# Delta-rule attention followed by a SiLU feed-forward: the output projection by seven products of blocks in place of eight, and what is moved for it

## The chip, the cores and the metric

The kernel runs on one core of a Trainium2 chip. The metric is the device time of one execution in microseconds; lower is better. Before the change it is 801.19 us, the median of three runs (799.85 to 801.63). The engines are called PE (TensorE), DVE (VectorE), ACT (ScalarE), POOL (GpSimd) and SP (the engine whose queue issues all DMAs here).

## The reference

There are 4 sequences (B), 8 heads (H), 768 tokens (S) and heads of 48 (D). For every sequence and head a 48x48 state is carried through the tokens:

```
k_n = k / (norm(k) + 1e-6);  state = 0
for t in range(S):
    y[t]  = q[t] @ state
    v_old = k_n[t] @ state
    state = state + beta[t] * outer(k_n[t], v[t] - v_old)
```

The outputs of the 8 heads of a token stand side by side (8 x 48 = 384) and go through a feed-forward, with w_in of 384x2048 and w_out of 2048x384:

```
h = x @ w_in
g = h * sigmoid(h)
out = g @ w_out            # 3072 x 384
```

Inputs and output are float32, but w_in and w_out reach the kernel as float64.

## The kernel before

**Tiling.** The 768 tokens are cut into 6 chunks of 128, and a chunk of one sequence is a unit; the 24 units are counted chunk by chunk. A chunk goes through four stages:

- *Preparation* (`prepare`), sequence by sequence: k and q are transposed on PE (`turn`, L369), scores are made from them (`score`, L392), scaled and masked on ACT and DVE into the tile `ap` (L402, L408), and the diagonal 32x32 blocks go out to DRAM and come back in another layout (`g`, L436 and L444). Then k is scaled into `bkb` and v in place, both on POOL.
- *Inversion* (`invert`): the 32x32 triangular blocks of all heads are inverted together on DVE, 30 steps of two instructions (L470, L474), each needing the one before. The result goes out (`up`, `low`, L485) and comes back into `xe` and `xi` (L488).
- *Solve* (`solve`): small products on PE merge the blocks and solve for Z (`zbufs`), update the state (`pu`) and give the outputs (`pyc`), in ten steps over the four sequences that overlap each other. DVE adds into `vf` (L558), updates the state (L616) and ACT and DVE copy `xT`, the transposed input of the feed-forward; its last rows come by six small DMAs a sequence (L653).
- *Feed-forward* (`feed_forward`), for each half of the chunk (two sequences): `hidden` makes 8 times two blocks of 128 hidden features for 256 tokens (L702), with SiLU on ACT into `gT` (L712); `project` then makes the output of each sequence from 16 blocks (L722), which ACT scales by 0.5 (L728) and SP stores (L730). The products of both use a pool of two PSUM banks (`psM`).

**Order.** The order of each engine's instructions is written out by hand: `pin` orders each compute instruction behind the one before it on its engine, and `in_line` does so for all DMAs, which share one queue of SP. So an instruction that waits holds up everything emitted after it on its engine. The feed-forward of chunk c is a generator, `pieces`; each step of it is a piece (three blocks of L702 or two of L722). The main loop runs preparation, inversion and solve of chunk c + 1 and takes pieces of chunk c in between, so that PE has work while the other engines make the next chunk. The last chunk's feed-forward stands alone at the end. Squares and norms of the k of chunk c + 2 (`squares`, `norms`, on ACT and DVE) are emitted behind solve of chunk c + 1.

**Weights.** A weight comes in as raw float64 and is narrowed to float32 in three steps on ACT, DVE and POOL (`narrow`, L164 to L180). There are eight pieces of w_in and eight of w_out. A raw piece needs a place of 6 KB a partition: the halves of `w_outs` not yet written, buffers of `gT`, a tile `spare`, and for pieces 2, 3, 6 and 7 of w_out two of the four buffers of `ap`. `fill`, `until` and `more` deal out the steps while chunk 0 is solved and chunk 1 prepared. `busy` (L274) puts idle products on PE in these stages.

**Buffers.** k has 5 buffers and q 4; q of the next chunk is loaded in preparation (`load_q`, L127), right after the block stores of its sequence. Z has four tiles of its own.

Of the kernel before, what the change touches and what calls it, by code (L numbers as in the profile page):

```python
# [21 lines left out]
def kernel(  # L22
# [85 lines left out]
    NQ, NK, NBK = 4, 5, 5  # L108
    qbufs = [const.tile([P, NP, 2, W], FP32, name=f"qb{i}") for i in range(NQ)]
    kbufs = [const.tile([P, NP, 2, W], FP32, name=f"kb{i}") for i in range(NK)]  # L110
    bkbufs = [const.tile([P, NP, 2, W], FP32, name=f"bkb{i}") for i in range(NBK)]
    vfs = {}
# [12 lines left out]
    def load_q(i):  # L125
        if i < N:
            in_line(nc.sync.dma_start(out=packed(qbufs[i % NQ]), in_=chunk_of(q, i)))  # L127
# [8 lines left out]
    for t in kbufs[:B] + qbufs:  # L136
        pin(nc.vector.memset(t[:, :, :, D:W], 0.0))
# [60 lines left out]
    def fetch_w_in(i):  # L198
        if i < 4:
            raw = room(1 - i // 2, i % 2)  # L200
        elif i < NWI - 1:
            raw = mlp.tile([P, SIZE], U32, name="raw", tag="gT", bufs=3)[:]
        else:
            raw = spare[:]
        raw = raw.rearrange("p (a f) -> p a f", a=NKT)
        for at, row, rows in ROWS:
            step = row(1) - row(0)
            src = moe_w_in[row(0) : row(0) + rows, i * WF : (i + 1) * WF].bitcast(U32)
            pitch = src.ap[0][0]
            src = bass.AP(  # L210
                tensor=src.tensor, offset=src.offset,
                ap=[[pitch, rows], [pitch * step, NKT], [1, 2 * WF]],
            )
            in_line(nc.sync.dma_start(out=raw[at : at + rows], in_=src))
        raws[i] = raw.rearrange("p a (f j) -> p a f j", j=2)

    raws = {}
    spare = const.tile([P, SIZE], U32, name="spare")
# [6 lines left out]
    def fetch_w_out(i):  # L225
        if i in (0, 1, 4):
            raw = room(1, min(i, 1))
        elif i == 5:
            raw = spare[:]
        else:  # L230
            k = i % 2
            if k not in places:
                places[k] = work.tile([P, SIZE], U32, name="raw_out", tag="ap", bufs=4)
            raw = places[k][:]
# [14 lines left out]
    for t in kbufs[B:] + bkbufs:  # L249
        nc.gpsimd.memset(t[:, :, :, D:W], 0.0)  # L250
# [9 lines left out]

    HH = HB * H
    xis = [const.tile([P, HH, W], FP32, name=f"xi{i}") for i in range(2)]
    xe = const.tile([W + T, BH, T], FP32, name="xe")

    zbufs = [const.tile([P, NP, 2, W], FP32, name=f"z{i}") for i in range(B)]
    for t in zbufs:
        nc.gpsimd.memset(t[:, :, :, D:W], 0.0)
# [26 lines left out]
    def squares(c):  # L294

        sums[c] = small.tile([P, BH], FP32, name="ss", bufs=1)[:]
        for b in range(B):
            sq = packed(zbufs[b])
# [59 lines left out]
    def turn(i, *rooms):  # L358

        b, c = units[i]  # L360
        kb, qb = kbufs[i % NK], qbufs[i % NQ]
# [84 lines left out]
    def invert(c):  # L446
# [39 lines left out]

        def move(to, src, j, mine):
            in_line(nc.sync.dma_start(out=to, in_=src[mine, j].rearrange("n s t -> s n t")))  # L488

        for hf in range(2):  # L490
            mine = slice(hf * HH, (hf + 1) * HH)
            for j in range(0, NB, 2):
                move(xe[T * j : T * (j + 1), mine, :], low, j, mine)
# [5 lines left out]
    xTs = {}  # L499

    def solve(c, us):
# [6 lines left out]
        ys, pzs, pys, third = {}, {}, {}, {}  # L508
# [5 lines left out]
        for g in range(2 if c == 0 else 0):  # L514
            thirds = work.tile([P, HB, NKT, 2, W], FP32, name="thirds", tag="gx"[g], bufs=1)
            pin(nc.gpsimd.memset(thirds[:], 0.0))
            for n in range(HB):
                third[g * HB + n] = thirds[:, n]

        def merge(g, second):  # L520
# [3 lines left out]
            for n in range(HB):  # L524
                x = g * HB + n
                for h in range(H):
                    for k in range(2):
                        even, odd = slice(W * k, W * k + T), slice(W * k + T, W * (k + 1))
                        if second:
                            to, left, right = even, ys[g][odd, n * H + h, :], xis[g][odd, n * H + h, T:W]  # L530
# [10 lines left out]
            else:  # L541
                ys[g] = work.tile([P, HH, T], FP32, name="y")
                pin(nc.scalar.copy(ys[g][T:W], pm[T:W]))
                pin(nc.vector.tensor_copy(out=ys[g][W + T : P], in_=pm[W + T : P]))
# [76 lines left out]
        def new(x):  # L621
# [29 lines left out]
            for e in range(2):  # L651
                for a in range(NKT):
# [3 lines left out]
                    ))  # L656

# [38 lines left out]
    def hidden(c, hf):  # L696

        for f in range(NFF // 2):
# [15 lines left out]
            ))  # L714
            yield

    def project(c, b, room=(psM, "m")):

        po = bank(*room, "po")
        for f in range(NFF):  # L720
# [5 lines left out]
            if f == NFF - 1:  # L726
                o = mlp.tile([P, DM], FP32, name="o")
                pin(nc.scalar.mul(o[:], po[:, 0:DM], 0.5))  # L728
                row = b * S + c * C
                in_line(nc.sync.dma_start(out=out[row : row + C, :], in_=o[:]))  # L730
            if f % 2 == 1:
                yield

    def feed_forward(c):
        for hf in range(2):
            yield from hidden(c, hf)
            for b in range(hf * HB, (hf + 1) * HB):
                yield from project(c, b)
# [8 lines left out]
    def prepare(c, us):  # L747

        for b in range(B):
# [7 lines left out]
            load_q(i + NQ)  # L757
            block_in(i)
            load_k(i + B)
            scale(i)  # L760
# [41 lines left out]
    def fill(n):  # L802

        ops = []
        while len(ops) < n and queue:
            piece = queue[0]
            piece.begin()
            if len(queue) > 1 and piece.done >= 2:
# [49 lines left out]
    for n, _ in enumerate(solve(0, us)):  # L858
        fill(2)
        if n == 3:  # L860
            more(2)
            more(3)
        if n == 8:
            more(4, ("out", 1))
# [4 lines left out]
    until(("in", 7))  # L869
    fetch_w_out(5)  # L870
    queue.append(Piece(("out", 5), narrow_w_out(5)))
# [3 lines left out]
    more(6, ("out", 2))  # L875
    more(7, ("out", 3))
    for n in range(2):
        go(prep)
        go(pieces, 3)
        fill(6)  # L880
    for n in range(2):
        until(("out", 6 + n))
        go(prep)
        go(pieces, 2)
    inv = invert(1)
    go(pieces, 6)
    for _ in range(20):
# [4 lines left out]
    go(pieces, 8)  # L892
    for n, _ in enumerate(solve(1, us)):
        go(pieces, 2 if n in (1, 2) else 1)
    squares(2)
    norms(2)
# [5 lines left out]
    for c in range(1, NCH):  # L902
        if c + 1 < NCH:
            us = []
            for n, _ in enumerate(prepare(c + 1, us)):
                go(pieces)
            go(pieces, 4)
            inv = invert(c + 1)
            n = 0
            for _ in inv:  # L910
                n += 1
                if n % 5 in (1, 3, 4):
                    go(pieces)
            go(pieces, 8)
            for n, _ in enumerate(solve(c + 1, us)):
                go(pieces, 2 if n in (1, 2) else 1)
            if c + 2 < NCH:
                squares(c + 2)
                norms(c + 2)
# [35 lines left out]
```

## Time and profile before

| | |
|---|---|
| median of 3 runs | 801.19 us |
| the profiled execution, its own time | 800.27 us |
| its span, from the first to the last instruction | 798.6 us |
| mean granted clock of TensorE | 0.974 |
| busy: PE, weight loads (PEld) | 760.3, 572.2 us |
| busy: DVE, ACT, POOL | 339.4, 231.1, 82.3 us |
| L702 (hidden) | 1152 instructions |
| L722 (output projection) | 768 instructions, for 384 products of 128x128 by 128x384: each product of float32 is two instructions |

The page gives busy times by engine, 40 slices of the span in tenths, and the chain of work that ended last, followed back from the end. A line of a group gives source line, engine, operation, output and inputs with their shapes, the number of instructions, busy time and the mean duration of one, and then the engine's idle time just before such instructions, with what ended it. In the chain in order of time each line has a start, a length and the work; a timeline is the same for one engine, with waits in brackets.

### The profile page before, as it was taken

Reading aid. Unit: us, or ns where it says so; the run is one execution under the profiler, and the core shown is the slowest. Engines: PE = TensorE matmul, PEld = TensorE weight load, DVE = VectorE, ACT = ScalarE, POOL = GpSimd, SP = SyncE. Lnnn points to the kernel's source line nnn. Section 1 sums busy time; section 2 is a strip of 40 time slices with the busy share of each in tenths; the row PEclk is TensorE's granted clock in tenths of the full one; section 3 lists DMA queues with packets and bytes.
Section 4 is the critical chain, followed back from the end, with each engine's and each line's share of the span. In section 5 each row is a group of like instructions: output and inputs, shape, how many; then the busy total and the mean of one; then the engine's idle time right before and its main releaser. Section 6 shows DMA issues by size and latency. Waiting matters only on the chain.

```text
span 798.6 us, 15397 instructions
## 1 busy us (share of the span) xinstructions
PE 760.3 (95%) x6326; PEld 572.2 (72%) x6326; DVE 339.4 (42%) x892; ACT 231.1 (29%) x502; POOL 82.3 (10%) x102
## 2 busy tenths in 40 slices
PE   7449798999999999999999999999999999999998
PEld 5336576678778688768678868678868778767684
DVE  5886779561254732424732424642425732100000
ACT  5533566121234113314113314113314113211020
POOL 5005246100020000030000030000030000000000
PEclk8769998999999999999999999999999999999999
DMA  9798747321025140025140025140022040000000
GB/s 157 119 183 150 178 131 172 77 73 32 15 58 106 36 103 2 12 60 106 37 103 2 10 61 103 40 100 6 10 61 44 16 107 2 11 22 0 21 1 20
DMA packets 155062, 50.85 MB, mean 64 GB/s; under 512 B 142544, under 2 KB 147536, under 8 KB 154992
## 3 DMA queue, kind: packets, MB, share of 16 engines
q1 hardware_dynamic: 154992, 49.87, 30.2%
q8 instruction: 50, 0.82, 0.4%
q14 instruction: 20, 0.16, 0.1%
HBM read 34.70 MB, written 14.16 MB: 61 GB/s over the span
## 4 chain that ended last, share of the span: by engine, by line
PE 83%; DVE 6%; DMA 5%; ACT 2%; SPq 2%; issue 1%; POOL 0%; ACTq 0%; DVEq 0%
PE phid L702 28%; PE po L722 28%; PE pa L392 5%; PE pz L567 4%; PE pw L274 3%; PE pt L369 3%; PE pyc L626 2%; PE ph L551 2%; PE pyc L598 2%; DMA qb<-in_q_dram 2%; PE px L534 2%; PE py L534 2%; PE pu L609 1%; DVE x L474 1%; DVE rank L470 1%
## 5 line engine op out<-in xcount | busy, mean ns | idle before, releaser
L702 PE MATMUL phid<-xT,w_in 128*128 128x256 f32 x1152 | 268.6, 386 | 1.3 <-ACT gT L712 0.8
L722 PE MATMUL po<-w_out,gT 128*128 128x384 f32 x768 | 254.8, 489 | 0.0
L702 PEld LDWEIGHTS phid<-xT,w_in 128*128 128x128 f32 x1152 | 215.0, 191 | 39.3 <-issue 7.0
L722 PEld LDWEIGHTS po<-w_out,gT 128*128 128x128 f32 x768 | 144.1, 190 | 97.2 <-issue 2.7
L712 ACT ACTIVATE gT<-phid 128x512 f32<-128x512 f32 x96 | 57.2, 598 | 155.3 <-PE phid L702 155.3
L408 DVE SCALAR_TENSOR_TENSOR ap<-pa,g,above 128x128 f32<-128x128 f32 x192 | 58.2, 376 | 46.8 <-ACT ap L402 46.4
L474 DVE TENSOR_TENSOR x<-x,rank 128x30 f32<-128x30 f32 (+9 forms) x180 | 59.7, 331 | 7.4 <-ACT x L463 1.1
L470 DVE TENSOR_TENSOR rank<-g,x 128x30 f32<-128x30 f32 (+9 forms) x180 | 59.7, 332 | 6.1
L392 PE MATMUL pa<-kq 48*128 48x256 f32 x384 | 54.2, 409 | 4.6 <-ACT ap L402 2.9
L728 ACT ACTIVATE o<-po 128x384 f32<-128x384 f32 x24 | 11.8, 491 | 158.1 <-PE po L722 158.1
L402 ACT ACTIVATE ap<-pa,g 128x128 f32<-128x128 f32 x144 | 41.6, 366 | 37.5 <-PE pa L392 33.8
L392 PEld LDWEIGHTS pa<-kq 48*128 48x128 f32 x384 | 38.5, 196 | 18.0 <-issue 9.6
L567 PEld LDWEIGHTS pz<-vf,xi 64*64 64x64 f32 x768 | 37.2, 138 | 9.8 <-issue 8.6
L345 POOL TENSOR_TENSOR bkb<-kb,g 128x384 f32<-128x384 f32 x24 | 20.0, 840 | 221.4 <-issue 158.6
L567 PE MATMUL pz<-vf,xi 64*64 64x48 f32 x768 | 41.7, 224 | 0.4 <-ACT raw L169 0.3
L558 DVE TENSOR_TENSOR vf<-vf,pz 64x384 f32<-64x384 f32 x24 | 13.4, 558 | 63.6 <-PE pz L567 37.6
L585 ACT COPY z<-pz 64x384 f32<-64x384 f32 x48 | 22.7, 473 | 57.8 <-PE pz L567 47.0
L558 DVE TENSOR_TENSOR vf<-vf,ph 128x384 f32<-128x384 f32 x20 | 11.1, 555 | 63.8 <-PE ph L551 63.8
L274 PE MATMUL pw<-state,ident 128*128 128x384 f32 x80 | 30.9, 532 | 4.0 <-DVE state L139 2.8
L369 PE MATMUL pt<-ident,qb 128*128 128x128 f32 x96 | 16.5, 300 | 15.2 <-DMA qb<-in_q_dram 15.2
L575 PE MATMUL pz<-z,ap 64*64 64x48 f32 x384 | 27.9, 224 | 0.0
L431 POOL MEMSET x<- 128x1024 f32 x6 | 5.7, 955 | 200.5 <-DMA up<-x 200.5
(104 smaller groups left out, 600.5 us busy)
## 6 DMA issues: line engine op xcount, KB each, us to landing
kb<-in_k_dram SPq DMA_DIRECT2D x24, 192.0 KB, 3.2
qb<-in_q_dram SPq DMA_DIRECT2D x24, 192.0 KB, 3.4
vf<-in_v_dram SPq DMA_DIRECT2D x24, 192.0 KB, 3.5
out_dram<-o SPq DMA_DIRECT2D x24, 192.0 KB, 1.9
blocks<-ap SPq DMA_DIRECT2D x96, 32.0 KB, 1.7
g<-blocks SPq DMA_DIRECT2D x24, 128.0 KB, 2.6
up<-x SPq DMA_DIRECT2D x6, 512.0 KB, 2.6
low<-g SPq DMA_DIRECT2D x6, 512.0 KB, 2.8
```

What stands on the lines that cost most here:

```text
L274: done = pin(nc.tensor.matmul(pw[:, 0:DM], lhsT=ident[:], rhs=states[B - 1][:].rearrange("p a w -> p (a w)")[:, 0:DM], start=True, stop=Tr ...
L369: pin(nc.tensor.transpose(pt[:, p * C : (p + 1) * C], src[:, p].rearrange("p e w -> p (e w)"), ident[:]))
L392: u["last"] = pin(nc.tensor.matmul(pa[e][:, pp * 2 * C : (pp + 1) * 2 * C], lhsT=kq[rows, 2 * g + pp, 0, :], rhs=kq[rows, 2 * g + pp, :, : ...
L402: copied = pin(nc.scalar.activation(out=ap[:, h, 0, :], in_=pa[e][:, at : at + C], func=ACTF.Copy, scale=bt[:, h : h + 1],))
L408: masked = pin(nc.vector.scalar_tensor_tensor(out=ap[:, h, j:2, :], in0=pa[e][:, at + j * C : at + 2 * C].rearrange("p (j t) -> p j t", j= ...
L470: pin(nc.vector.tensor_tensor(out=tv, in0=g[:, 0:m, m : m + 1].to_broadcast([P, m, n]), in1=x[:, m : m + 1, m + 1 : T].to_broadcast([P, m, ...
L474: yield pin(nc.vector.tensor_tensor(out=x[:, 0:m, m + 1 : T], in0=x[:, 0:m, m + 1 : T], in1=tv, op=ALU.add))
L534: pin(nc.tensor.matmul(pm[to, at : at + T], lhsT=left, rhs=right, start=True, stop=True))
L567: yield pin(nc.tensor.matmul(pzs[x][rows, h, :], lhsT=xis[x // HB][rows, x % HB * H + h, :], rhs=vs[x][rows, h, :], start=True, stop=True,))
L702: pin(nc.tensor.matmul(ph[:, j * GT : (j + 1) * GT], lhsT=w_in[:, a, (2 * f + j) * P : (2 * f + j + 1) * P], rhs=xTs[c, hf][:, a, :], star ...
L712: pin(nc.scalar.activation(out=gTs[f // FG][:, f % FG, :], in_=ph[:], func=ACTF.Silu, scale=0.5))
L722: pin(nc.tensor.matmul(po[:, 0:DM], lhsT=gTs[f // 2 // FG][:, f // 2 % FG, at : at + C], rhs=w_outs[f // HFF][:, f % HFF, :], start=(f == ...
```

## The change

Write G for the hidden features of half a chunk, cut into blocks by parity of the feature block (j) and sequence (n), and W for w_out cut by parity (j) and half of the output columns (m). The output of half a chunk is a 2x2 product of these blocks, eight products of blocks. For chunks 1 to 5 `combine` makes it from seven, each a chain of 8 blocks with 192 columns (L813), out of sums of blocks: three sums over W are made once into `sums_of_w` and a fourth in place (`sum_w`), and four sums over G in each half into the two parts of `sums_of_g`, in three groups of feature blocks each (`sum_g`, S1 to S4, on DVE). Products gather in two PSUM banks, px and py; ACT copies partial results out while a bank goes on adding, and DVE adds later ones to the output tile (L821). Both sequences are stored at the end. Chunk 0 keeps `project`.

The room for the sums is made so: q is loaded into the tiles of Z, after the output of the sequence in solve, for the next chunk; k and bkb have 4 buffers; `spare` lies in `sums_of_g`; `thirds` and `xe` of chunk 0 lie in `sums_of_w`, and `xe` of later chunks and `y` in tiles that the inversion has left; raw pieces 4, 6 and 7 of w_out lie in `sums_of_w` and `spare`. Squares and norms of chunk c + 2 move into solve of chunk c + 1, the squares behind its sixth step and the norms behind its seventh, and four of five steps of the inversion take a piece instead of three.

```diff
-    NQ, NK, NBK = 4, 5, 5
+    NK = NBK = NZ = B
...
     def load_q(i):
-            in_line(nc.sync.dma_start(out=packed(qbufs[i % NQ]), in_=chunk_of(q, i)))
+            in_line(nc.sync.dma_start(out=packed(zbufs[i % NZ]), in_=chunk_of(q, i)))
...
-    spare = const.tile([P, SIZE], U32, name="spare")
+    sums_of_g = const.tile([P, 2, NFF // 2, C], FP32, name="sums_of_g")
+    spare = sums_of_g[:].rearrange("p k f t -> p (k f t)").bitcast(U32)[:, 0:SIZE]
+    HM = DM // 2
+    sums_of_w = [const.tile([P, NFF // 2, HM], FP32, name=f"sums_of_w{i}") for i in range(3)]
...
     def fetch_w_out(i):
-        if i in (0, 1, 4):
+        if i in (0, 1, 5):
             raw = room(1, min(i, 1))
-        elif i == 5:
-            raw = spare[:]
+        elif i in (4, 7):
+            raw = sums_of_w[2 if i == 4 else 0][:].rearrange("p f m -> p (f m)").bitcast(U32)
+        elif i == 6:
+            raw = spare
         else:
-            k = i % 2
+            k = int(i == 3)
...
     def new(x):
...
+            load_q((c + 1) * B + x)
...
     def hidden(c, hf):
...
+            if c > 0 and f % FG == 1 and f >= FG:
+                for which in (S1, S2):
+                    sum_g(which, f // FG - 1)
             yield
...
+    def sum_w():
+        n = HFF // 2
+        for k, left, right, op in (
+            (0, (1, 1), (0, 1), ALU.subtract), (1, 0, (0, 0), ALU.add), (2, (1, 0), 1, ALU.subtract),
+            (None, (0, 1), (0, 0), ALU.subtract),
+        ):
+            for i in range(2):
+                of = [
+                    quarters(i, *x) if isinstance(x, tuple) else sums_of_w[x][:, n * i : n * (i + 1)]
+                    for x in (left, right)
+                ]
+                to = of[0] if k is None else sums_of_w[k][:, n * i : n * (i + 1)]
+                yield pin(nc.vector.tensor_tensor(out=to, in0=of[0], in1=of[1], op=op))
+
+    S1, S2, S3, S4 = (
+        (0, (0, 1), (1, 1), ALU.add), (1, 0, (0, 0), ALU.subtract),
+        (0, (0, 0), (0, 1), ALU.subtract), (1, (1, 0), 1, ALU.subtract),
+    )
+
+    def sum_g(which, g):
+        k, left, right, op = which
+        fs = group(g)
...
+        pin(nc.vector.tensor_tensor(out=sums_of_g[:, k, fs], in0=of[0], in1=of[1], op=op))
...
+    def combine(c, hf):
+        o = mlp.tile([P, 2, DM], FP32, name="o", bufs=1)
+        px, py = bank(psM, "m", "px"), bank(psM, "m", "py")
...
+        def chain(to, a, b, start=False):
+            for f in range(NFF // 2):
...
+                pin(nc.tensor.matmul(
+                    to, lhsT=at, rhs=quarter(f, *b) if isinstance(b, tuple) else sums_of_w[b][:, f],
+                    start=start and f == 0, stop=f == NFF // 2 - 1, skip_group_check=True,
+                ))
+                if f % 4 == 3:
+                    yield
...
+        yield from steps(chain(px[:, left], (0, 0), (0, 0), True), (S1, NG - 1), (S2, NG - 1))
+        yield
+        yield from steps(chain(px[:, right], (1, 1), 2))
+        pin(nc.scalar.mul(o[:, :, left], px[:, 0:DM].rearrange("p (n m) -> p n m", n=2), 0.5))
+        yield
+        yield from steps(chain(py[:, left], 0, (0, 1), True))
+        pin(nc.scalar.mul(o[:, 1, right], py[:, left], 0.5))
+        yield
+        yield from steps(chain(px[:, left], 1, 1), *((S3, g) for g in range(NG)))
+        pin(nc.scalar.mul(o[:, 0, right], px[:, left], 0.5))
+        yield
+        yield from steps(chain(py[:, right], (1, 0), (1, 0)), *((S4, g) for g in range(NG)))
+        add_half(o[:, 0, left], py[:, right])
+        yield
+        yield from steps(chain(px[:, left], 0, 0))
+        add_half(
+            o[:, 1].rearrange("p (n m) -> p n m", n=2),
+            px[:, left].unsqueeze(1).to_broadcast([P, 2, HM]),
+        )
+        yield
+        yield from steps(chain(py[:, left], 1, (1, 1)))
+        add_half(o[:, 0, right], py[:, left])
+        for n in range(2):
+            row = (hf * HB + n) * S + c * C
+            in_line(nc.sync.dma_start(out=out[row : row + C, :], in_=o[:, n]))
+        yield
...
     def prepare(c, us):
...
             block_out(i, us[b])
-            load_q(i + NQ)
             block_in(i)
-            load_k(i + B)
             scale(i)
+            load_k(i + B)
             size(i)
...
         if n == 3:
             more(2)
             more(3)
+            more(4)
         if n == 8:
-            more(4, ("out", 1))
+            more(5, ("out", 1))
...
-    until(("in", 7))
-    fetch_w_out(5)
-    queue.append(Piece(("out", 5), narrow_w_out(5)))
+    more(6, ("in", 7))
+    more(7)
...
-    more(6, ("out", 2))
-    more(7, ("out", 3))
-    for n in range(2):
+    for n in range(4):
         go(prep)
-        go(pieces, 3)
-        fill(6)
-    for n in range(2):
-        until(("out", 6 + n))
-        go(prep)
-        go(pieces, 2)
+        go(pieces, 3 if n < 2 else 2)
+        fill(6 if n == 0 else 3)
     inv = invert(1)
-    go(pieces, 6)
+    for n in range(6):
+        until(("out", min(7, n + 2)))
+        go(pieces)
...
             for _ in inv:
                 n += 1
-                if n % 5 in (1, 3, 4):
+                if n % 5 in (0, 1, 3, 4):
                     go(pieces)
-            go(pieces, 8)
+            go(pieces, 7)
             for n, _ in enumerate(solve(c + 1, us)):
                 go(pieces, 2 if n in (1, 2) else 1)
-            if c + 2 < NCH:
-                squares(c + 2)
-                norms(c + 2)
+                if n == 5 and c + 2 < NCH:
+                    squares(c + 2)
+                if n == 6 and c + 2 < NCH:
+                    norms(c + 2)
```

## The prediction

> **What bounds the kernel now.** I read the page first: busy shares, slices, chain.
>
> ```profile
> PE 760.3 (95%) x6326; PEld 572.2 (72%) x6326; DVE 339.4 (42%) x892; ACT 231.1 (29%) x502; POOL 82.3 (10%) x102
> ...
> PE   7449798999999999999999999999999999999998
> ...
> PEclk8769998999999999999999999999999999999999
> ...
> PE 83%; DVE 6%; DMA 5%; ACT 2%; SPq 2%; issue 1%; POOL 0%; ACTq 0%; DVEq 0%
> ```
>
> TensorE is busy 760.3 of 798.6 us, and from the seventh slice on at full granted clock. The share is an average, so I asked for busy time by stage: 300 to 320, 354 to 474 and 594.8 to 712.4 us each show PE busy for the whole stretch. Of the 38 us in which it is not, all but about 9 lie before 110 us, in the loading of weights, and 3.5 of those 9 are the last store. So for chunks 1 to 5 the time is the sum of PE's own work, whatever DVE, ACT and SP do. The chain of waits, in order of time, gives that work's true rates, since it runs from end to end without overlap:
>
> ```profile
> 415.83 3.54 PE ph L551 x32
> ...
> 712.37 20.72 PE phid L702 x96
> 733.09 20.64 PE po L722 x64
> ```
>
> A 384-column instruction (L722) takes 20.64/64 = 322.5 ns, a 256-column one (L702) 20.72/96 = 215.8 ns: 0.8336 ns a column and 2.4 ns besides. The means of the groups (486 ns, 379 ns) hold the latency of overlapping instructions and are no rate. L551 matters for a different reason: 96 columns would be 82 ns by that line but take 3.54/32 = 110.6 ns, with a weight load of 128 columns before each. So a full weight load costs about 110 ns of throughput, and is hidden wherever a product is longer.
>
> **The products.** Of chunks 1 to 5, half a chunk (two sequences) has 64 instructions of 384 columns (2 sequences x 16 blocks x 2 passes). Afterwards it has 7 products x 8 blocks x 2 passes = 112 of 192 columns. The trace has no 192-column row. Between 110.6 (load bound) and 215.8 ns, the line through the two long rows gives 192 x 0.8336 + 2.4 = 162.5 ns; I take it, since it is well above 110.6. Then 112 x 162.5 = 18.2 us against 20.64: 2.44 us less, ten times: **24.4 us**. One rule of the Trainium skill speaks against it (TensorE: Matmul & The Clock Gate, Part 3, what overlaps and what doesn't): weight loads overlap matmuls in flight only if they use other row groups. All rows are used here. By the rule a product would cost load plus stream, 110 + 160 = 270 ns against 110 + 320 = 430, or 30.2 against 27.5 us: 27 us slower in all. The L702 row decides: same full-row loads, yet 215.8 ns between products where the serial sum would be 110 + 216. The rule doesn't hold for this stream. If instead the load's 190 ns latency set the pace, the half would be 112 x 190 = 21.3 us, 6.4 us slower over ten; L551 at 110.6 ns with loads of that same latency speaks against it. These are the far ends.
>
> **The sums on DVE.** Each half adds 12 sums over gT: eight of 128x384, four of 128x256. Nearest rows:
>
> ```profile
> L616 DVE TENSOR_TENSOR state<-state,pu 64x192 f32<-64x192 f32 x40 | 14.1, 352 | 21.7 <-PE pu L609 21.0
> ...
> L474 DVE TENSOR_TENSOR x<-x,rank 128x240 f32<-128x240 f32 x12 | 4.9, 408 | 0.4
> ...
> L474 DVE TENSOR_TENSOR x<-x,rank 128x130 f32<-128x130 f32 x12 | 3.5, 295 | 0.4
> ```
>
> From 130 to 240 elements it is 1.03 ns an element: 0.56 us for 384, 0.42 for 256, so 8 x 0.56 + 4 x 0.42 = 6.2 us. Three additions out of PSUM (192, 384, 192) are 0.41 + 0.61 + 0.41 = 1.4 us. Ten halves: 76 us; the eight sums over w_out (128x768, about 1 us by L176's 958 ns) 8 us. DVE goes from 339 to about 423 us of a 770 us span, 55%. Averaged, PE covers it. Two places have little cover.
>
> *Inversion.* It is a DVE chain of some 22.5 us in which PE has only pieces of the feed-forward.
>
> ```profile
> 374.10 2.42 DVE L408 SCALAR_TENSOR_TENSOR ap<-pa,g,above 128x128 f32<-128x128 f32 x8 [2.57 <-ACT ap L402]
> 382.71 0.36 DVE L461 COPY x<-g 128x16 f32<-128x16 f32 x3 [6.19 <-DMA g<-blocks]
> ...
> 392.00 0.40 DVE L474 TENSOR_TENSOR x<-x,rank 128x234 f32<-128x234 f32 x1
> ```
>
> I count from PE's last score (374.2). PE: nine hidden pieces (11.85 us in the chain), then 7 products x 2.6 us: the next hidden block starts at +30.05, and needs the bank of px, which DVE frees with its addition after the sixth product. DVE: starts at +8.5, reaches the end of the 234 row at +18.2, and in order adds four sums before it (2.1), three (1.6), two steps (1.8), three sums (1.6), two steps (1.8), an addition (0.4), two steps (1.75), the addition (0.6): +29.9. The margin is 0.15 us. The second bank comes free at +32.8 against a need at +32.65. The sums themselves are early: the one that the sixth product needs is begun at +20.3 and used at +24.9. I charge 0.7 us a chunk, four chunks: **2.8 us**. Bounds: 0, and 4 us a chunk if each sum waits or costs half more. Inversion ends 6.8 us later on DVE, at +37.8. Its DMAs (up, low, then 12 on SP) took 10 us to issue; merges stand at +53, since 25 pieces now sit in the inversion in place of 19: no loss.
>
> *Solve.* The squares and norms of the chunk after next move into it, from behind it. Norms are 15 small instructions, 3.5 us in the trace (458.74 to 462.2), and three sums (1.6 us) stand before them. Behind them in DVE's queue waits the addition to vf of the last sequence (0.56), which PE needs. From the end of PE's output product of the first sequence, DVE takes 1.3 + 1.6 + 3.5 + 0.6 = 7.0 us; PE reaches the need after piece, old, pz, pu, output, piece, old: 1.49 + 0.89 + 1.06 + 0.60 + 0.89 + 1.49 + 0.89 = 7.3. Barely covered: 0.3 us a chunk, **1.2 us**, up to 2 a chunk. The four squares on ACT (1.8 us) end before the next step's copies.
>
> **Moved DMAs.** q of the next chunk was loaded in preparation; now SP issues each 192 KB load in solve, after a sequence's six xT transfers (SP spent 17.7 us on 24 in solve). Four issues of 0.45 us make 19.5; out stores, v loads and the first block stores queue behind. The first q is issued near 446.5 of the old clock and used no earlier than 459: hidden. The last lands 10 us before use. k loads now wait for the scaling of their own buffer (0.84 us on POOL, idle there): hidden. Outputs leave as two stores after the last product in place of one by one; only at the very end is that uncovered: **0.6 us**, one more issue and landing.
>
> **The first stages.** Raw pieces 4, 6 and 7 of w_out no longer sit in ap's buffers or behind another piece.
>
> ```profile
> 122.08 4.15 PE L702 MATMUL phid<-xT,w_in 128*128 128x256 f32 x18
> 126.16 0.70 PE L392 MATMUL pa<-kq 48*128 48x256 f32 x2
> 129.43 3.07 PE L392 MATMUL pa<-kq 48*128 48x256 f32 x14 [2.57 <-ACT ap L402]
> 132.43 5.38 PE L702 MATMUL phid<-xT,w_in 128*128 128x256 f32 x12
> ```
>
> Scores wait for ACT, which waits for a raw piece in flight (4.0 us), then for ap buffers that POOL still adds from (2.7 us), and the clock falls. From 112.84 to 142.87 PE needs 4 x 1.93 + 10 x 1.3 = 20.7 us and takes 30. Afterwards the four scores (2.42 each) and the narrowing of only four pieces (about 3.07 each by the means of L166, L172, L176) plus 1.4 of gaps stand on DVE from 114.1: the last ends at 137.5, not 142.4. I take **5 us** gained; bounds 0 (the same narrowing still sets it) and 9.3. The later w_out pieces are narrowed under the output pieces that use them, one per piece. Further, the 1.4 us that PE lost at 224 to 235 waiting for norms of chunk 2 goes: **1.4 us**. The sums over w_out (6 before solve, 2 in preparation) meet an idle DVE.
>
> **The sum**, against the profiled execution: span 798.6 - 24.4 - 5 - 1.4 + 2.8 + 1.2 + 0.6 = 772.4 us. The median 801.19 lies 2.6 above that span (the profiled run's own time, 800.27, 1.7), so **775.0**.
>
> **Rivals.**
> *DVE becomes the bound in inversion and solve* (chance 0.16). For: the margins of 0.15 and 0.3 us. Against: any slip is bounded by the sums' 7.6 us a half. At 3 us more a chunk, four chunks: 787.
> *The start gains nothing* (0.12). DVE was busy 34 of 40 us from 100 to 140, and the number of narrowings is the same. 775 + 5 = 780.
> *Loads set the pace* (0.07), the other side: products run at the 190 ns latency of a load. The half costs 21.3 us, and the sum is 775 + 24.4 + 6.4 = 806. It decides from about 187 ns a product on, where seven halves of products cost 0.26 us more a half than eight did, and eat the 2.6 us that the other terms leave.
> *Products come out as stated but stall on each other* (0.03): a chain into px must wait for ACT's copy of px. One chain of 2.6 us into py lies between; if each half lost 2.4 us there, the time would be 799.
>
> **How the numbers follow.** The likeliest, 0.62, is 775.0, itself from 769 (start at its upper bound, stalls nil) to 781. The range takes in the DVE and start rivals and stops short of the load rival: 768 to 788. A measurement of this kernel can tell about 0.2%, 1.6 us. Faster: 0.62 + 0.16 + 0.12 + 0.02 = 0.92; slower 0.07; same 0.01.
>
> **What would show it.** L722's successor: chain blocks of 112 instructions in 18.2 us after 712 (old clock), with no other engine near; 21 us there is the load rival. A chunk's period of 120.3 us falls to about 116. In each, PE idle under 1.5 us, named as waiting for DVE's addition (px) or vf. The first output product starts near 138, not 142.9. Wrong it would be if sums ran behind PE (idle PE with DVE named in the waits), if weight loads show on PE's path, or if q's landing appears ahead of the transposes.

## The result, and the profile after

The changed kernel takes 770.31 us (median of four runs, 768.87 to 772.96), the kernel before, on the same chip, 801.41 (799.85 to 803.52): a ratio of 0.9614, with an interval of 0.958 to 0.9648. The forecast was 775.0, with a range of 768 to 788. The profiled execution took 770.21 us, with a span of 768.5 and a mean granted clock of 0.977.

The page of the kernel after, from its busy times, its slices and its chain:

```profile
PE 730.4 (95%) x6806; PEld 630.0 (82%) x6806; DVE 411.8 (54%) x1050; ACT 233.3 (30%) x512; POOL 83.6 (11%) x95
...
PE   7549799899999999999999999999999999999997
...
PEclk8859999999999999999999999999999999999999
...
PE 88%; DVE 4%; DMA 3%; SPq 2%; issue 1%; ACT 1%; POOL 1%; ACTq 0%; DVEq 0%
```

PE is busy 29.9 us less and the span is 30.1 us shorter, so PE still sets the time. It has 480 more instructions (6806 against 6326) and takes less for them. DVE has 72 us more to do (411.8 against 339.4) and stands on less of the chain than before: 4% against 6%.

The end of the kernel, where only the feed-forward is left, in the chain of waits in order of time (start, length, work):

```profile
725.68 20.72 PE phid L719 x96
746.40 5.20 PE px L813 x32
751.60 2.60 PE py L813 x16
...
762.00 2.61 PE py L813 x16
```

Seven products of 16 instructions take 18.21 us, where L722 took 20.64. That is 162.6 ns an instruction; 162.5 was worked out ahead from the two longer rows. The hidden half (20.72) is unchanged to the hundredth.

The chunks in the middle, by stage: from the last score of one chunk to the last score of the next, first for the kernel before, then for the one after (busy time of each engine, with the number of instructions; then clock, DMA share and GB/s):

```profile
354.28:474.56 120.28, 120.28 (x1057) 92.21 (x1057) 50.20 (x144) 32.91 (x75) 7.45 (x10) 1.00 0.25 53
```

```profile
247.91:363.31 115.40, 115.40 (x1154) 104.54 (x1153) 62.84 (x174) 33.20 (x78) 7.48 (x10) 1.00 0.26 56
```

A chunk is shorter by 4.88 us, twice 2.44 (the next two take 115.40 us too), and PE is busy for the whole of it, both before and after. The 12.6 us that DVE has more in a chunk, the moved loads and the moved norms cost PE nothing here.

The start, in PE's timeline of the kernel after (in brackets the idle time before, and what ended it):

```profile
133.96 7.90 PE L742 MATMUL po<-w_out,gT 128*128 128x384 f32 x24
142.98 1.56 PE L742 MATMUL po<-w_out,gT 128*128 128x384 f32 x4 [1.11 <-POOL w_out L181]
146.34 11.88 PE L742 MATMUL po<-w_out,gT 128*128 128x384 f32 x36 [1.80 <-POOL w_out L181]
...
170.22 1.99 PE L719 MATMUL phid<-xT,w_in 128*128 128x256 f32 x8 [1.64 <-ACT gT L729]
```

The waits of the scores on `ap` are gone, and with them the fall of the clock. PE comes to the output pieces at 133.96 (before at 142.87), then waits for pieces of w_out twice and for ACT once. The hidden block behind that last wait starts at 170.22, before at 174.79: 4.57 us are left of the 8.9. Of these, 0.9 lie ahead of the first score of chunk 1 (111.94 against 112.84), where executions of the same code differ by more than that (the table among the experiments); 3.67 lie behind it.

All of it: 24.4 (ten halves at 2.44), 4.57 of the start, and 1.45 more up to the first score of chunk 2 (229.21 against 235.23, so 6.02 in all), less 0.4 at the end, where the last two stores lie behind the last product (3.9 us from PE's end to the end of the span, before 3.5). That is 30.0 of the 30.1 us.

### The profile page after: what moved, and what is told of

Its sections match the earlier page's. It is cut to its first block, busy times and chain, and to the rows that moved or that the text cites. A ratio compares the mean times of both kernels' runs of the same rounds, so it can differ in the third digit from the quotient of the medians.

```text
span 768.5 us, 16585 instructions
## 1 busy us (share of the span) xinstructions
PE 730.4 (95%) x6806; PEld 630.0 (82%) x6806; DVE 411.8 (54%) x1050; ACT 233.3 (30%) x512; POOL 83.6 (11%) x95
## 4 chain that ended last, share of the span: by engine, by line
PE 88%; DVE 4%; DMA 3%; SPq 2%; issue 1%; ACT 1%; POOL 1%; ACTq 0%; DVEq 0%
PE phid L719 31%; PE px L813 14%; PE py L813 11%; PE pa L399 6%; PE pz L583 4%; PE pt L376 3%; PE po L742 3%; PE pw L276 3%; PE pyc L642 3%; PE pyc L614 2%; PE ph L567 2%; DMA z<-in_q_dram 2%; PE px L551 2%; PE py L551 2%; PE pu L625 2%; DVE x L481 1%
## 5 line engine op out<-in xcount | busy, mean ns | idle before, releaser
L719 PE MATMUL phid<-xT,w_in 128*128 128x256 f32 x1152 | 260.7, 382 | 2.2 <-ACT gT L729 1.6
L795 DVE TENSOR_TENSOR sums_of_g<-gT 128x384 f32<-128x384 f32 (+1 forms) x60 | 29.2, 509 | 57.9 <-ACT gT L729 47.3
L813 PE MATMUL py<-w_out,sums_of_g 128*128 128x192 f32 x320 | 56.8, 329 | 0.0
L813 PE MATMUL px<-sums_of_w,sums_of_g 128*128 128x192 f32 x320 | 56.8, 329 | 0.0
L813 PEld LDWEIGHTS px<-sums_of_w,sums_of_g 128*128 128x128 f32 x320 | 52.2, 190 | 1.4 <-issue 1.4
L813 PEld LDWEIGHTS py<-w_out,sums_of_g 128*128 128x128 f32 x320 | 52.2, 190 | 0.4
L399 PE MATMUL pa<-kq 48*128 48x256 f32 x384 | 51.0, 401 | 0.2 <-DVE ap L415 0.2
L742 PE MATMUL po<-w_out,gT 128*128 128x384 f32 x128 | 44.7, 495 | 2.9 <-POOL w_out L181 2.9
L399 PEld LDWEIGHTS pa<-kq 48*128 48x128 f32 x384 | 36.9, 192 | 12.1 <-issue 8.1
L742 PEld LDWEIGHTS po<-w_out,gT 128*128 128x128 f32 x128 | 23.3, 190 | 18.4 <-POOL w_out L181 4.2
```

The source lines that it names most:

```text
L399: u["last"] = pin(nc.tensor.matmul(pa[e][:, pp * 2 * C : (pp + 1) * 2 * C], lhsT=kq[rows, 2 * g + pp, 0, :], rhs=kq[rows, 2 * g + pp, :, : ...
L719: pin(nc.tensor.matmul(ph[:, j * GT : (j + 1) * GT], lhsT=w_in[:, a, (2 * f + j) * P : (2 * f + j + 1) * P], rhs=xTs[c, hf][:, a, :], star ...
L742: pin(nc.tensor.matmul(po[:, 0:DM], lhsT=gTs[f // 2 // FG][:, f // 2 % FG, at : at + C], rhs=w_outs[f // HFF][:, f % HFF, :], start=(f == ...
L795: pin(nc.vector.tensor_tensor(out=sums_of_g[:, k, fs], in0=of[0], in1=of[1], op=op))
L813: pin(nc.tensor.matmul(to, lhsT=at, rhs=quarter(f, *b) if isinstance(b, tuple) else sums_of_w[b][:, f], start=start and f == 0, stop=f == ...
```

## The experiments

Each kernel is the changed one with the edit shown. The time after "before" is that of the kernel before on the same chip. The changed kernel itself gave 770.31, and 771.43 (766.93 to 775.49) in six later runs.

The first stages differ from execution to execution. In the first eight kernels of this table (down to e7) the order of instructions is the same up to the first score of chunk 1, yet this score begins anywhere from 109.57 to 118.19 us. A wait of PE named "issue" at the first merge (3.0 us in one execution, 0.8 in another, none in e6) is a part of this; the rest was not traced. From that score to the end the two profiles of the changed kernel agree within 0.3 us, so the last column tells small differences better than the medians do (profiled executions, us):

| kernel | first score of chunk 1 | span | from there to the end |
|---|---|---|---|
| after | 111.94 | 768.5 | 656.6 |
| r1, the changed kernel again | 111.46 | 767.8 | 656.3 |
| e1 | 111.37 | 803.5 | 692.1 |
| e2 | 111.59 | 737.5 | 625.9 |
| e3 | 116.08 | 772.5 | 656.4 |
| e4 | 114.52 | 787.7 | 673.2 |
| e6 | 109.57 | 770.7 | 661.1 |
| e7 | 118.19 | 791.4 | 673.2 |
| e5 | 114.53 | 774.1 | 659.6 |
| v1 | 111.73 | 769.0 | 657.3 |
| v2 | 108.86 | 763.3 | 654.4 |
| before | 112.84 | 798.6 | 685.8 |

**The eighth product back** (e1_eighth), to see whether the gain is the product or idle time that would fill anyway:

```diff
         yield from steps(chain(px[:, right], (1, 1), 2))
...
         yield
+        yield from steps(chain(px[:, right], (1, 0), (1, 0)))
         yield from steps(chain(py[:, left], 1, (1, 1)))
```

> An eighth product of blocks (16 instructions of 192 columns, into the unused right half of px) is added to every half of chunks 1 to 5; its result is not read. If the time is the sum of PE's work: 16 x 162.5 ns = 2.60 us a half, ten halves, +26.0 us on the changed kernel's 770.3, so 796, and 18.2 becomes 20.8 us in the last block of products. If PE stands partly on DVE or on weight loads, the extra product fills idle time and the rise is well under 26.

Measured: 805.17 us in one run (before 800.73), span 803.5: 35.0 above the kernel after. The chain of waits of this kernel, in the inversion, and below it the row of its waits on PE (total, times, longest):

```profile
274.68 0.57 DVE o L821
275.25 0.04 issue
275.29 2.87 PE px L813 x16
```

```profile
PE px L813 <- DVE o L821: 7.0, 10, 1.2
```

Each of the ten products costs its 2.60, as expected, plus 0.70 of waiting and 0.27 because the product behind a stop takes 2.87: together 35.7. The table gives 35.5. No idle time filled: the product is worth what PE takes for it. The wait is new. The product writes the right half of px while DVE still reads the left half of that bank, and PE goes on only 0.04 us after DVE is done. In the changed kernel products alternate between px and py where DVE reads, and PE never waits there: where a product stands matters, not the number of products alone.

**Narrow products** (e2_narrow96), to see at which length weight loads take over:

```diff
+                rhs = quarter(f, *b) if isinstance(b, tuple) else sums_of_w[b][:, f]
+                cols = HM if f == 0 else HM // 2
                 pin(nc.tensor.matmul(
-                    to, lhsT=at, rhs=quarter(f, *b) if isinstance(b, tuple) else sums_of_w[b][:, f],
+                    to[:, 0:cols], lhsT=at, rhs=rhs[:, 0:cols],
```

> Seven of the eight blocks of every product run on 96 of the 192 columns (left out: the rest of the output). If a weight load of 128 columns costs 110 ns of throughput, the instruction takes 110.6 ns, not the 82.4 of the straight line: a product is 2 x 162.5 + 14 x 110.6 = 1.87 us and the last half's seven 13.1 us. If loads are free at any width: 1.48 us and 10.4. If the load's 190 ns latency counts for anything, more than 13.1. The whole: 770.3 - 10 x (18.2 - 13.1) = 719, and somewhat more where DVE's sums now come late.

Measured: 739.22 us in one run, span 737.5. A product in the chain at the end; PE's timeline in the inversions of the first and the second chunk with seven products; and the window behind the second wait (busy times by engine, then the granted clock, here 0.50):

```profile
727.95 1.89 PE py L815 x16
```

```profile
273.05 2.13 PE L815 MATMUL py<-w_out,sums_of_g 128*128 128x192 f32 x16 [2.69 <-DVE o L823]
...
381.66 3.94 PE L815 MATMUL py<-w_out,sums_of_g 128*128 128x192 f32 x16 [2.70 <-DVE o L823]
```

```profile
382.00:385.00 3.00, 3.00 (x15) 3.00 (x14) 2.83 (x8) 0.00 (x0) 0.00 (x0) 0.50 0.00 0
```

The product takes 1.89 us. Two of its 16 instructions are full ones (0.325), so the 14 narrow ones take (1.89 - 0.325) / 14 = 111.8 ns; their columns alone would be 82. With L551 (110.6 ns, also 96 columns) this fits a weight load that costs 110 to 112 ns of throughput and is hidden at 192 columns with 50 ns to spare; no run changed the load alone, so another floor of the same size is not excluded. The rival in which loads set the pace at 190 ns falls here as in the chain above. The time itself missed its expectation of 719 by some 20 us: shorter products let PE run ahead of DVE in the inversion, and PE waits 2.7 us for DVE's addition in each of four chunks (10.8 in all). In three of the four the clock then falls to half, and the next product takes 3.6 to 3.9 us; behind the first wait, as long as the others, the clock stays at 1.00 and the product takes 2.13. These slow stretches, which reach into the hidden block behind the product, make up most of the rest.

**Sums only once** (e3_sums_once), and **sums twice** (e4_sums_twice), for the rival in which DVE becomes the bound:

```diff
+        if which[0] in made_sums.setdefault(g, []):
+            return
+        made_sums[g].append(which[0])
...
```

> The sums over G (S1 to S4) are made only once, for the first half of chunk 1, and left out afterwards: 114 of 120 instructions, about 57 us of DVE, go. If PE covers them, as the bound by PE says: no change, within 1 us of 770.3. If the sums hold PE up as the prediction charged (0.7 us a chunk in the inversion, 0.3 in solve): 766.

Measured: 771.39 us (768.06 to 774.25), a ratio to the kernel before of 0.9619 (0.9578 to 0.966): the changed kernel's own. Three chunks take 115.40 us each, as in the changed kernel, and the table has 656.4 against 656.6. (The edit makes S1 and S2 once and S3 and S4 not at all, since S3 and S4 have the same places as S1 and S2: 6 sums of 120 are left.) What DVE spends on the sums costs nothing.

```diff
-        pin(nc.vector.tensor_tensor(out=sums_of_g[:, k, fs], in0=of[0], in1=of[1], op=op))
+        if which is S4:
+            sum_once(S3, g)
+        for _ in range(1 if which is S4 else 2):
+            pin(nc.vector.tensor_tensor(out=sums_of_g[:, k, fs], in0=of[0], in1=of[1], op=op))
...
```

> Every sum over G takes DVE twice its time (S1, S2, S3 issued twice, S3 a third time ahead of S4). In the changed kernel's trace DVE's addition after the sixth product ends 2.0 us before the next hidden block needs its bank, and the addition to vf in solve 0.7 us before its need. Twice the sums bring 4.7 us ahead of the first and 1.4 ahead of the second: PE should lose about 2.7 and 0.7 us a chunk, +12 to 14 us, 783. If DVE's idle 46% were what counts: no change.

Measured: 787.68 us (785.93 to 789.43), a ratio of 0.9836 (0.9792 to 0.988). PE's waits that the changed kernel does not have:

```profile
PE px L825 <- DVE sums_of_g L809: 7.1, 4, 2.0
...
PE py L825 <- DVE o L833: 4.2, 4, 1.1
PE pz L583 <- DVE vf L574: 3.1, 3, 1.0
```

14.4 us in eleven waits, and some 0.2 for each restart, make the 16.6 us of the table (12 to 14 expected). They stand in the stages that the prediction named, the inversion and solve. In solve it is the addition to vf, as named. In the inversion it is not the bank of px, which the prediction had as the place: the sixth product waits for a sum (7.1 us), and the seventh, into py, for DVE's addition behind the fifth (4.2 us). The first of these is in part made by the edit itself, which puts the repeated S3, read by the sixth product, between the parts of S4. So the cover is real and is used up within one more round of sums. That nothing is lost now is no general slack of DVE.

**The old start** (e5_old_start): raw pieces of w_out in the places and the order of before. Its core:

```diff
-        if i in (0, 1, 5):
+        if i in (0, 1, 4):
             raw = room(1, min(i, 1))
-        elif i in (4, 7):
-            raw = sums_of_w[2 if i == 4 else 0][:].rearrange("p f m -> p (f m)").bitcast(U32)
-        elif i == 6:
+        elif i == 5:
             raw = spare
         else:
-            k = int(i == 3)
+            k = i % 2
...
-    more(6, ("in", 7))
-    more(7)
+    until(("in", 7))
+    fetch_w_out(5)
+    queue.append(Piece(("out", 5), narrow_w_out(5)))
...
+    more(6, ("out", 2))
+    more(7, ("out", 3))
```

> The changed kernel with the raw pieces of w_out in their old places and the old order of narrowing in chunk 1's preparation; all else as changed. If the start gains by these places, as the prediction says: +5 us, 775; by the traces the hidden block of chunk 0's second half began its middle at 174.8 and begins it at 170.2, so +4.6. If the gain came from elsewhere (fewer memsets, Z's tiles): 770.

Measured: 775.83 us (773.83 to 776.21), a ratio of 0.9703 (0.9626 to 0.9781). PE's timeline of this kernel:

```profile
130.81 2.96 PE L397 MATMUL pa<-kq 48*128 48x256 f32 x14 [2.16 <-ACT ap L407]
133.70 5.49 PE L717 MATMUL phid<-xT,w_in 128*128 128x256 f32 x12
```

The wait on `ap` is back, and twelve hidden instructions take 5.49 us for 2.7 again. The block that started at 170.22 starts at 175.81, 5.6 later. Of this, 2.6 lie ahead of the first score, among them 1.1 of a longer "issue" wait near 81 us; the scatter of the first stages is larger than that. From the first score to the block it takes 61.28 us, against 58.28 and 58.02 in the two profiles of the changed kernel and 61.95 in the kernel before. So the places of the raw pieces and the order of narrowing are worth 3.0 to 3.3 us there; whether they also gain anything ahead of the first score is not shown.

**Squares and norms behind solve again** (e6_norms_after):

```diff
...
-                if n == 5 and c + 2 < NCH:
-                    squares(c + 2)
-                if n == 6 and c + 2 < NCH:
-                    norms(c + 2)
+            if c + 2 < NCH:
+                squares(c + 2)
+                norms(c + 2)
```

> Squares and norms back behind solve. In chunk 1 PE then waits again for the norms of chunk 2, as it did for 1.4 us. In later chunks only three pieces (3.9 us) and a transposition now lie between solve and the scores that need the norms, against 12 pieces before; DVE's last copy of solve, reduces and norms take 0.6 + 1.9 + 3.5 us and the squares start them 1 us late. Expected: 1.5 us in chunk 1 and about 1 us in each of three more, +4 us. If they are covered anyway: no change.

Measured: 772.42 us (770.59 to 778.13), a ratio of 0.968 (0.9605 to 0.9754). A chunk takes 115.92 us instead of 115.40, half of it a wait of 0.26 for DVE's addition behind the norms. In chunk 1 PE's wait for the norms is back, and the clock falls behind it. PE's timeline there, and the window behind the score:

```profile
228.16 2.01 PE L399 MATMUL pa<-kq 48*128 48x256 f32 x16 [1.44 <-DVE kq L385]
230.10 2.93 PE L719 MATMUL phid<-xT,w_in 128*128 128x256 f32 x6
```

```profile
230.00:232.00 2.00, 2.00 (x7) 1.54 (x6) 2.00 (x8) 1.04 (x4) 2.00 (x3) 0.50 0.82 156
```

From the first score of chunk 1 to the last of chunk 2 this costs 3.0 us, and three chunks cost 0.52 each: 4.5 by the table, against 4 expected. The agreement is partly luck, since some 1.6 us of it is the slow clock, which was not counted, and a later chunk loses half of the 1 us expected. By the medians alone, with the scatter of the first stages in them, the move can't be told from nothing.

**Three pieces in five steps of the inversion** (e7_inv_three), the old pace:

```diff
-                if n % 5 in (0, 1, 3, 4):
+                if n % 5 in (1, 3, 4):
                     go(pieces)
-            go(pieces, 7)
+            go(pieces, 8)
```

> The inversion takes a piece at three of five steps again, and eight pieces behind it, so five pieces fewer (6.5 us) lie between its start and the merges, and five more behind solve. By the changed kernel's trace the second xe lands at about 297 and the merge that needs it begins at 301; 6.5 us earlier it would wait some 2.5 us: four chunks, +10 us. If the inversion had slack as in the kernel before (5.7 us): no change, or up to 1 us.

Measured: 789.82 us (786.48 to 793.15), a ratio of 0.9885 (0.9769 to 1.0001). The expected cause, late merges, is not there. PE's timeline in an inversion, and the window behind it:

```profile
284.01 4.50 PE L813 MATMUL py<-w_out,sums_of_g 128*128 128x192 f32 x16 [2.60 <-DVE o L821]
```

```profile
284.00:286.60 2.60, 2.58 (x8) 2.59 (x9) 2.43 (x8) 0.00 (x0) 0.00 (x0) 0.50 0.00 0
```

DVE's additions are emitted with the pieces. At three pieces in five steps, more steps of the inversion stand ahead of an addition in DVE's queue, and PE waits 2.6 us for it, for the bank of py. Then the clock is at 0.50, and the product takes 4.50 us for 2.6. The waits (2.60, 2.06, 2.09 and 2.38 us: 9.1) and the stretched products (4 x 1.9) make 16.7 us; four chunks longer by 4.0 to 4.5 each make the same, and the table has 16.6. The rest of the 22.9 us by which this profile's span is longer lies ahead of the first score of chunk 1. So the pace of the inversion, to which the prediction gave no term of its own, is needed for the gain: without it some 16.6 of the 24.4 us are given back.

**The start again** (v1_v_first): loads of v ahead of raw pieces 6 and 7.

```diff
-    more(6, ("in", 7))
-    more(7)
+    until(("in", 7))
     for n in range(B, 2 * B):
         load_v(n)
+    more(6)
+    more(7)
```

> The loads of v for chunk 1 are issued ahead of the raw pieces 6 and 7 of w_out. In the changed kernel POOL waits for v at 128 us (behind these pieces in the queue), narrows piece 5 late, and ACT waits 5.6 us for it; PE then waits 1.1, 1.8 and 1.6 us between 134 and 170. If v is what is late, most of these 4.5 us go: 767. If the raw pieces then come late by as much: no change, 770.

Measured: 771.13 us (770.74 to 772.49), a ratio of 0.9654 (0.9592 to 0.9717): no gain (657.3 in the table, against 656.6 and 656.3). POOL has its v 4 us earlier (117.48 against 121.73 for the first scaling), but ACT still waits 4.65 us for POOL's step of piece 5. The order of loads isn't it.

**Raw piece 5 in a place of its own** (v2_five_in_w1), beside the changed kernel once more (r1_after_again). Piece 6 of w_out is narrowed into the half of `w_outs` in which raw piece 5 lies, so ACT waits for POOL to finish piece 5 (5.63 us at 135.01 in the kernel after):

```diff
-        if i in (0, 1, 5):
+        if i in (0, 1):
             raw = room(1, min(i, 1))
-        elif i in (4, 7):
-            raw = sums_of_w[2 if i == 4 else 0][:].rearrange("p f m -> p (f m)").bitcast(U32)
+        elif i in (4, 5, 7):
+            raw = sums_of_w[{4: 2, 5: 1, 7: 0}[i]][:].rearrange("p f m -> p (f m)").bitcast(U32)
...
-            if len(queue) > 1 and piece.done >= 2 and piece.name != ("out", 5):
+            if len(queue) > 1 and piece.done >= 2:
```

> Raw piece 5 of w_out goes into the second tile of sums_of_w in place of the half of w_out that pieces 6 and 7 are narrowed into. In the changed kernel piece 6's first step waits 5.6 us on ACT for piece 5's addition on POOL, because it writes over piece 5's raw bytes; with v loaded early nothing was gained, so it is this place and not v that is late. Without it ACT starts piece 6 once its load has landed, the last score comes some 4 us earlier and PE's waits of 1.1 and 1.8 us for w_out go: 767. If PE then only waits elsewhere before chunk 1's solve, 770 as before.

> The changed kernel itself, unaltered, on the chip that runs v2, so that the two are compared there: 770 us.

Measured: 769.89 us (765.02 to 774.2), a ratio of 0.9607 (0.9565 to 0.9649), against 771.43 and 0.9636 (0.9592 to 0.9681) for the changed kernel. PE's timeline with the new place:

```profile
132.09 20.91 PE L742 MATMUL po<-w_out,gT 128*128 128x384 f32 x64
...
165.02 3.29 PE L719 MATMUL phid<-xT,w_in 128*128 128x256 f32 x14 [1.66 <-ACT gT L729]
```

Both waits for POOL are gone. From the first score to the hidden block it takes 56.16 us, against 58.02 in the later profile of the changed kernel (r1): 1.9 us, of PE's 2.9. The 4 us expected at the last score are not there: these scores begin 17.5 us after the first ones, in r1 16.7. The medians differ by 1.5 us and their ranges overlap, so by time alone this version is not shown to be faster.

## Why the prediction came out as it did

**The products.** Right to the hundredth: 2.44 us a half, 24.4 in all. The length was read from the line through two longer rows, and that line holds down to 192 columns. The rule that weight loads overlap only across row groups (the Trainium skill, TensorE: Matmul & The Clock Gate, Part 3) would have made each half 2.7 us slower by the prediction's sum; the row L702 decided against it, and the seven products in a row at 2.60 confirm it. The same part of that page also has loads pulled ahead when they go to a background weight buffer, so it is this one line of it that the rows contradict. Two small slips of the sum changed nothing: the terms besides the products leave 1.8 us, not 2.6, so the rival of slow loads would turn the sign from about 186 ns, not 187; and DVE has 72 us more to do, not 84.

**The stalls in the inversion and in solve.** This is the step that failed: 2.8 and 1.2 us were charged, and both are nil (without the sums, in e3, a chunk takes the same 115.40 us). The stages were right, the count was too tight, and I charged a loss where my own count still left a margin in the first bank (0.15 us) and in solve (0.3). In the inversion, the timelines of DVE and, below, of PE show why:

```profile
267.51 1.36 DVE L795 TENSOR_TENSOR sums_of_g<-gT 128x384 f32<-128x384 f32 x3
268.78 0.40 DVE L477 TENSOR_TENSOR rank<-g,x 128x238 f32<-128x238 f32 x1
...
273.34 0.35 DVE L821 SCALAR_TENSOR_TENSOR o<-py,o 128x192 f32<-128x192 f32 x1
...
275.40 0.56 DVE L821 SCALAR_TENSOR_TENSOR o<-px,o 128x384 f32<-128x384 f32 x1
```

```profile
272.60 2.76 PE L813 MATMUL px<-sums_of_w,sums_of_g 128*128 128x192 f32 x16
275.20 2.76 PE L813 MATMUL py<-w_out,sums_of_g 128*128 128x192 f32 x16
277.80 18.29 PE L719 MATMUL phid<-xT,w_in 128*128 128x256 f32 x84
```

Three sums take 1.36 us, the next instruction starting 1.27 after the first of them, and not the 1.6 us counted: they do not read each other, and one of 384 elements is followed 0.47 us later by the next, though it lasts about 0.55. The counted value came from rows of a chain in which each instruction needs the one before. With the inversion's start 0.16 us earlier and shorter steps, the addition that frees px is done at 275.96, 28.05 us after the last score and not 29.9; PE needs the bank at 277.8. The margin is 1.8 us, not 0.15. It is 1.8 also where the sums are left out (e3): this addition follows its product at once.

The hand-over that gives way first is another one, which the prediction set against no need. The seventh product writes the left half of py, and the addition behind the fifth reads the right half of it. By the prediction's own sum this addition ends at +27.5 and the seventh product begins at +27.45. Here it ends at 273.69, 1.5 us before the product begins (275.20). In e2, e4 and e7 this is where PE waits, and it goes on 0.06 us after the addition's end.

In solve the addition to vf is done at 328.63, which is 6.65 us after the output product (7.0 counted), and PE needs it 7.33 us after it (7.3 counted): a margin of 0.7, not 0.3. The chain, and the addition in DVE's timeline:

```profile
321.09 0.89 PE pyc L642 x16
321.98 1.50 PE px L813 x8
...
329.31 1.06 PE pz L583 x16
```

```profile
328.07 0.56 DVE L574 TENSOR_TENSOR vf<-vf,pz 64x384 f32<-64x384 f32 x1
```

**The start.** Near in size (4.57 against 5, of which 3.67 behind the first score), and only about half of it by the way described, so the size was partly luck. The last scaling of `ap` ends at 139.9, which is 2.6 us before the 142.47 of the kernel before and not at the 137.5 expected, since ACT waits for raw piece 5. The rest lies on SP's queue, which I had not counted. SP's queue before, and after:

```profile
139.71 2.56 SPq L436 DMA_DIRECT2D blocks<-ap  x4
142.32 0.46 SPq L127 DMA_DIRECT2D qb<-in_q_dram  x1
143.61 0.31 SPq L444 DMA_DIRECT2D g<-blocks  x1
...
144.52 2.00 SPq L436 DMA_DIRECT2D blocks<-ap  x4
```

```profile
139.97 1.78 SPq L443 DMA_DIRECT2D blocks<-ap  x4
142.96 0.31 SPq L451 DMA_DIRECT2D g<-blocks  x1
```

Before, the scalings of the last two sequences ended 2.8 us apart (139.65 and 142.47), so the block stores of the last stood behind the stores of the third, its q load, and its load of g, which waits for those stores to land: the last stores were issued 2 us after their data was there. Now the third is scaled at 128.3 and SP is free when the fourth comes. The inversion starts 5.27 us earlier (145.45 against 150.72). Its first three copies take 1.06 us instead of 0.36, and 4.57 remain; why they do was not tried.

**The norms of chunk 2** gave 1.45 us (1.4 expected). **Moved loads** of q and k cost nothing: no wait of PE names them after chunk 0's own loads. **The last stores** cost 0.4, not 0.6.

**The sum.** The span came out at 768.5, not 772.4: 4.0 of stalls that weren't there, 0.2 less at the end and 0.4 less gained at the start. Another 0.8 is the step from span to median: 2.6 was taken over from the runs before, and it is 1.8 here. Of the rivals, loads as the bound and stalls between the chains are ruled out by the chain at the end. That one product holds up the next is real, but only with the eighth (e1), and there it is DVE's read of the bank and not ACT's copy. DVE as the bound is false for this kernel, and begins to be true at twice the sums (e4) or at the old pace of the inversion (e7). The start gained, by e5 3.0 to 3.3 us.

## What to carry to other kernels

Where one engine is busy without a gap, cost an edit by that engine's own rate, read off a stretch of the chain where it runs alone; group means would have given no usable number here. Then count, at each place where another engine must hand something back, when it is done and when it is needed, also where only the other half of a bank is read: the order of instructions in that other engine's queue decides, not its busy share (54% here, and one more round of sums already cost 17 us). A positive margin is a reason to charge nothing as the likeliest value and to widen the range upward.

## What the runs showed that had not been expected

- A wait of PE can cost more than its length, and its length alone does not tell when. Behind waits of 0.65 to 2.00 us in e1 and e4 the clock stays at 1.00 and PE loses 0.2 to 0.3 us besides. Behind all four waits of e7 (2.06 to 2.60 us) and three of the four in e2 (2.69 to 2.70) it is granted at 0.50, and the next product takes 1.5 to 2.05 us longer; behind the first of e2, also 2.69, it stays at 1.00. In e6 it falls to 0.50 behind a wait of 1.44 us, while the kernel before has one of 1.45 in the same place and keeps 1.00. What else decides it was not tried.
- Two halves of one PSUM bank are not independent in this program: a product into one half began 0.04 us after DVE had finished reading the other (0.70 us of waiting on the mean of ten, e1). Whether the chip or the program's own waits ask for this was not told apart.
- A 96-column instruction with a full weight load takes 110 to 112 ns, where its columns alone would take 82, although a load lasts 190 ns by its group's mean.
- DVE sums of 384 elements that do not read each other's output come 0.47 us apart, though each lasts 0.55.
- The first stages vary: the first score of chunk 1 begins at 109.6 to 118.2 us in eight executions with the same code up to there, of which a wait of PE on "issue" at the first merge (up to 4.6 us, none in e6) is only a part.
